# Tiled attention before a feed-forward chain: the last 192 queries of a head as two chunks of 96 on partition 0, products with v in one block per pair half

## The chip, the cores and the metric

The kernel runs on one core of a Trainium2 chip. The metric is the device time of one execution in microseconds (us). A core has TensorE (PE, which multiplies matrices, with a loader for its stationary operand, PEld), VectorE (DVE), ScalarE (ACT), GpSimd (POOL) and a DMA-issuing engine (SP). PE reads SBUF and writes PSUM, which has eight banks of 512 fp32 columns by 128 partitions.

## The reference

```python
def _attn_ref(q, k, v, s):            # 4 batches, 8 heads, 576 positions, head size 64
    scores = scale * np.matmul(q, k.transpose(0, 1, 3, 2))
    cum = np.cumsum(np.maximum(s, 0.0), axis=-1)
    bias = -(cum[:, :, :, None] - cum[:, :, None, :])
    scores = np.where(causal, -1000000000.0, scores + np.minimum(bias, 0.0))
    ...
    attn = attn / (np.sum(attn, axis=-1, keepdims=True) + 1e-09)
    return np.matmul(attn, v).astype(np.float32)

def reference(**kwargs):
    ...
    x = np.ascontiguousarray(attn_out.transpose(0, 2, 1, 3)).reshape(B * S, H * D)
    x = _moe_ref(x=x, **moe_kwargs)      # h = x @ w_in; (h - tanh(h)) @ w_out
    return _moe2_ref(x=x, **moe2_kwargs) # ((x @ w1) * (x @ w2) @ w3) @ w_out
```

## The kernel before

The first 440 us hold the attention, with half of the first feed-forward layer woven in, which ends near 490 us; the rest is feed-forward alone. Heads are worked in pairs (`Pair`): head e = 0 of a pair has its 64 components on partitions 0 to 63 of the tile `qk`, head e = 1 on 64 to 127. A pair half of kind "A" does queries 0 to 255, one of kind "B" queries 256 to 575. Queries are cut into five chunks, which begin at `CH0` = 0, 128, 256, 384, 448 and are 128 long. The fifth overlaps the fourth: only its rows from partition 64 on (`PLO`) are used, queries 512 to 575. A "B" half has three units (`UNITS`): B1 is chunk 3, B2 is chunk 4 with its first 512 keys, B3 is chunk 4's last 64 keys and chunk 2.

For each unit, `scores` multiplies queries by keys (per head one matmul with 64 contraction rows; PE runs each fp32 matmul as two passes), `minimum` adds the bias and takes a row's minimum on DVE, `exps` does the exponentials on ACT with row sums in `sums`. Seven steps later `transposes` turns the probabilities on PE, `BANKS` naming for each unit the key chunks and the query chunks whose blocks go side by side into a PSUM tile `pt`; `evacuate` copies it to the SBUF tile `pf`; `products` multiplies by v into the PSUM tile `pv`, head e = 0 into partitions 0 to 63 (64 stationary columns), e = 1 into 64 to 127. `invert`, `turn`, `store` and `spread` turn the reciprocals of the row sums (`ri`, 4 or 6 columns) on PE, write them to DRAM and read them back broadcast; `finish` multiplies `pv` by them into `xy`.

PSUM: the pool `ps_a` has five banks under one tag "s", shared by the scores, `pt`, `pv` and the turned reciprocals.

The order on PE is the order in which the code emits (`manual_schedule`). The function `at(step, order, fn)` fills a table of steps; each unit takes two steps, a pair (A and B) eight. In a step the transposes of one head come first, then `turn`, then scores, then feed-forward work (12 matmuls `h`, or 12 matmuls `y`, each of 256 columns), then `products`. Batch 0 comes first, four "A" halves, then four "B" halves; there (`p.first`) the bias and the mask are added on PE by extra matmuls, and exponentials read PSUM. Batches 1 to 3 follow as 12 pairs A, B. The other engines' order is chosen by the scheduler.

Of the kernel before, what the change touches and what calls it, by code (L numbers as in the profile page):

```python
# [8 lines left out]
F32 = mybir.dt.float32  # L9
# [21 lines left out]
CH0 = [0, 128, 256, 384, 448]  # L31
PLO = [0, 0, 0, 0, 64]
# [3 lines left out]
def tile_kernel(ctx: ExitStack, tc: tile.TileContext, qk, v, s, w_in, w_out, w1, w2, w3t, w_o2, outT):  # L36
# [65 lines left out]
    with ExitStack() as actx:  # L102
        def pool(name, bufs, **kw):
# [11 lines left out]
                 "B3": ((4, 512, S, 384), (2, 0, 384, 0))}  # L115
# [48 lines left out]
        def bias(p, i):  # L164
# [8 lines left out]
            if not p.first:  # L173
                t, lo, w = p.pr[i], PLO[i], min(P * (i + 1), S)
                for e in range(2):
                    c = cq[lo:, i, p.g[e]:p.g[e] + 1]
                    if i in (2, 3):
                        nc.gpsimd.tensor_scalar(out=t[lo:, e, :w], in0=p.cb[lo:, e, :w], scalar1=c, scalar2=0.0, op0=ALU.add, op1=ALU.min)  # L178
                    else:
                        nc.scalar.activation(t[lo:, e, :w], p.cb[lo:, e, :w], AF.Identity, bias=c)  # L180
# [6 lines left out]
        def causal(p, i):  # L187
            lo, w = PLO[i], min(P * (i + 1), S)
            dg = p.pr[i][lo:, :, P * i:w]
            nc.gpsimd.affine_select(out=dg, in_=dg, pattern=[[0, 2], [-1, w - P * i]], compare_op=ALU.is_ge,  # L190
                                    fill=-8e9, base=0, channel_multiplier=1)

        def scores(p, j):
            ps = [ps_a.tile([P, 512], F32, tag="s", name=f"s{p.n}_{j}_{e}") for e in range(2)]
            p.banks[j] = ps
            for i, k0, k1, o in UNITS[j]:
                for e in range(2):
                    x = p.raw[D * e:D * e + D]
                    latest[0] = nc.tensor.matmul(ps[e][:, o:o + k1 - k0], x[:, 0, CH0[i]:CH0[i] + P], x[:, 1, k0:k1],  # L199
                                                 start=(i, k0, k1, o) == UNITS[j][0] or not p.first, stop=not p.first, skip_group_check=p.first)  # L200
            if p.first:


                for e in range(2):
                    g = p.g[e]
                    todo = []
                    for i, k0, k1, o in UNITS[j]:
                        z, r = REL[i]
                        todo.append((ps[e][:, o:o + k1 - k0], pick[:, g:g + 1].broadcast_to([P, P]), rel2[z][:, r + k0:r + k1]))
# [6 lines left out]
        def minimum(p, j):  # L216
# [3 lines left out]
            if p.first:  # L220
                nm = p.nm
                for i, k0, k1, o in UNITS[j]:
                    lo = PLO[i]
                    c = 5 if i == 4 and not k0 else i
                    for e in range(2):
                        nc.vector.tensor_reduce(out=nm[lo:, e, c:c + 1], in_=p.banks[j][e][lo:, o:o + k1 - k0], op=ALU.max, axis=mybir.AxisListType.X)
                    if i == 4 and k0:
                        nc.vector.tensor_tensor(out=nm[lo:, :, 4:5], in0=nm[lo:, :, 4:5], in1=nm[lo:, :, 5:6], op=ALU.max)
                    if c < 5:
                        nc.vector.tensor_scalar(out=nm[lo:, :, c:c + 1], in0=nm[lo:, :, c:c + 1], scalar1=-0.125, scalar2=None, op0=ALU.mult)  # L230
                return
            for e in range(2):
                ps, nm = p.banks[j][e], p.nm[:, e]
                for i, k0, k1, o in UNITS[j]:
                    lo, t = PLO[i], p.pr[i][:, e]
                    part = i == 4 and not k0
                    nc.vector.tensor_tensor_reduce(  # L237
                        out=t[lo:, k0:k1], in0=ps[lo:, o:o + k1 - k0], in1=t[lo:, k0:k1], scale=-0.125,
                        scalar=nm[lo:, 5:6] if k0 else 3e38, op0=ALU.add, op1=ALU.min,
                        accum_out=nm[lo:, 5:6] if part else nm[lo:, i:i + 1])  # L240

        def exps(p, j):
            if p.sums is None:
                p.sums = a2.tile([P, 2, 4], F32, tag="sums", name=f"sums{p.n}", bufs=6)
                if not p.early:
                    nc.gpsimd.memset(p.sums[:D, :, 2:3], 1.0)
            for i, k0, k1, o in UNITS[j]:
                if i == 4 and not k0:
                    continue
                lo, c = PLO[i], i - p.i0  # L250
                for e in range(2):
                    t, m = p.pr[i][:, e], p.nm[lo:, e, i:i + 1]
                    if p.first:
                        if i == 4:
                            nc.scalar.activation(t[lo:, :512], p.banks["B2"][e][lo:, :512], AF.Exp, bias=m, scale=0.125, accum_out=p.sums[lo:, e, 3:4])  # L255
                        nc.scalar.activation(t[lo:, k0:k1], p.banks[j][e][lo:, o:o + k1 - k0], AF.Exp, bias=m, scale=0.125,
                                             accum_out=p.sums[lo:, e, c:c + 1])
                    else:
                        nc.scalar.activation(t[lo:, :], t[lo:, :], AF.Exp, bias=m, scale=-1.0, accum_out=p.sums[lo:, e, c:c + 1])  # L259
                if i == 4 and p.first:  # L260
                    nc.vector.tensor_add(p.sums[lo:, :, 2:3], p.sums[lo:, :, 2:3], p.sums[lo:, :, 3:4])

        def transposes(p, j, e):
            pt = ps_a.tile([P, 512], F32, tag="s", name=f"pt{p.n}_{j}_{e}")
            at, pieces = 0, []
            for kj, cs in BANKS[j]:
                beg = at
                for i in cs:
                    lo = PLO[i]
                    nc.tensor.transpose(pt[:, at:at + P - lo], p.pr[i][lo:, e, CH0[kj]:CH0[kj] + P], ident[lo:, lo:])  # L270
                    at += P - lo
# [9 lines left out]
        def products(p, j):  # L281
            got = [p.pf.pop((j, e)) for e in range(2)]
            if j in ("A", "B1"):
                if p.first and p.early:
                    p.pv = ps_y.tile([P, 512], F32, tag=f"y{p.n % 2}", name=f"pv{p.n}")
                else:
                    p.pv = ps_a.tile([P, 512], F32, tag="s", name=f"pv{p.n}")
            n = len(got[0][0])
            for z in range(n):
                for e in range(2):  # L290
                    kj, c, beg, end = got[e][0][z]
                    nc.tensor.matmul(p.pv[D * e:D * e + D, c:p.nq], p.vs[:, e, kj], got[e][1][:, beg:end],  # L292
                                     start=j in ("A", "B1") and z == 0, stop=j in ("A", "B3") and z == n - 1,
# [457 lines left out]
```

## Time and profile before

| what | value |
|---|---|
| runs | 1053.44, 1053.82, 1057.58 us, median 1053.82 |
| the profiled execution | 1053.08 us, its span 1051.3 us, mean granted TensorE clock 0.974 |
| busy of the span | PE 1001.3 us (95%), PEld 790.7 (75%), DVE 530.6 (50%), ACT 399.7 (38%), POOL 251.4 (24%) |
| the chain that ended last | PE 76%, DVE 10%, DMA 7%, ACT 4%, issue 2%, POOL 1% |
| transposes of the B halves (L270, `pt_B`) | 384 matmuls, 78.8 us busy |
| scores of the B halves (L199, `s_B`) | 256 matmuls, 64.1 us busy |

The span runs from the first to the last instruction, and the execution's own time is 1.8 us longer. Busy times of PE overlap from one matmul to the next, since matmuls are pipelined: what a matmul takes in a stream is read from the distance of the starts, not from its duration. The granted clock has two levels, 2.4 GHz (1.00) and 1.2 GHz (0.50); a mean over a stretch lies between.

### The profile page before, as it was taken

Reading aid. Unit: us, or ns where it says so; the run is one execution under the profiler, and the core shown is the slowest. Engines: PE = TensorE matmul, PEld = TensorE weight load, DVE = VectorE, ACT = ScalarE, POOL = GpSimd, SP = SyncE. Lnnn points to the kernel's source line nnn. Section 1 sums busy time; section 2 is a strip of 40 time slices with the busy share of each in tenths; the row PEclk is TensorE's granted clock in tenths of the full one; section 3 lists DMA queues with packets and bytes.
Section 4 is the critical chain, followed back from the end, with each engine's and each line's share of the span. In section 5 each row is a group of like instructions: output and inputs, shape, how many; then the busy total and the mean of one; then the engine's idle time right before and its main releaser. Section 6 shows DMA issues by size and latency. Waiting matters only on the chain.

```text
span 1051.3 us, 15383 instructions
## 1 busy us (share of the span) xinstructions
PE 1001.3 (95%) x5798; PEld 790.7 (75%) x5801; DVE 530.6 (50%) x1172; ACT 399.7 (38%) x978; POOL 251.4 (24%) x245
## 2 busy tenths in 40 slices
PE   6678799999999999999999999999999999999998
PEld 3345566666777777899877778888888888888898
DVE  8885554675555555553297674758412213122121
ACT  3454476765656564322233323223212112121121
POOL 3332365653333441100143321214101001000000
PEclk8978797999999999999999999999999999999999
DMA  6655664464222220205537453447910101001010
GB/s 208 208 183 203 206 186 135 152 194 140 91 77 91 83 92 14 69 21 167 175 120 240 160 196 99 165 141 269 363 70 1 41 0 41 1 1 41 1 41 21
DMA packets 46233, 123.64 MB, mean 118 GB/s; under 512 B 4976, under 2 KB 16912, under 8 KB 46160
## 3 DMA queue, kind: packets, MB, share of 16 engines
q1 hardware_dynamic: 41840, 106.94, 30.2%
q10 hardware_dynamic: 4320, 15.73, 4.5%
q8 instruction: 45, 0.74, 0.3%
q14 instruction: 28, 0.23, 0.1%
HBM read 92.09 MB, written 30.56 MB: 117 GB/s over the span
## 4 chain that ended last, share of the span: by engine, by line
PE 76%; DVE 10%; DMA 7%; ACT 4%; issue 2%; POOL 1%; SPq 0%; ACTq 0%; POOLq 0%; DVEq 0%
PE oc L98 9%; PE a L98 9%; PE b L98 9%; PE h L98 9%; PE y L391 8%; PE hb L98 6%; PE yb L98 6%; PE pt_B L270 5%; PE pv L292 4%; PE w3o L98 4%; PE s_B L199 3%; ACT pr L259 1%; DMA wf_d<-park_wout 1%; DVE cvt_w L76 1%; PE s_A L199 1%
## 5 line engine op out<-in xcount | busy, mean ns | idle before, releaser
L98 PEld LDWEIGHTS h<-xhl,win 128*128 128x128 f32 x864 | 110.0, 193 | 28.1 <-issue 14.1
L98 PE MATMUL h<-xhl,win 128*128 128x256 f32 x864 | 124.7, 292 | 2.9 <-DVE th L422 2.1
L698 DVE TENSOR_TENSOR pc<-b,pc 128x512 f32<-128x512 f32 (+1 forms) x40 | 25.5, 637 | 163.3 <-PE b L98 163.3
L98 PE MATMUL hb<-x,win 128*128 128x512 f32 (+1 forms) x480 | 106.3, 368 | 0.6 <-DMA win<-wf_d 0.6
L98 PE MATMUL a<-y,w 128*128 128x512 f32 (+1 forms) x480 | 106.4, 368 | 0.0
L98 PE MATMUL b<-y,w 128*128 128x512 f32 (+1 forms) x480 | 106.0, 368 | 0.0
L98 PE MATMUL yb<-ghb,wout 128*128 128x512 f32 (+1 forms) x320 | 97.3, 370 | 5.7 <-ACT ghb L60 3.8
L98 PE MATMUL oc<-phc,w3s 128*128 128x512 f32 (+1 forms) x320 | 96.7, 368 | 0.0
L98 PEld LDWEIGHTS hb<-x,win 128*128 128x128 f32 x480 | 84.0, 188 | 15.5 <-DMA win<-wf_d 0.8
L98 PEld LDWEIGHTS b<-y,w 128*128 128x128 f32 x480 | 84.3, 189 | 15.0
L98 PEld LDWEIGHTS a<-y,w 128*128 128x128 f32 x480 | 84.2, 189 | 14.9
L178 POOL TENSOR_SCALAR pr<-cb,cq 128x384 f32<-128x384 f32 (+1 forms) x48 | 85.9, 1807 | 21.5 <-PE pt_B L270 21.5
L270 PE MATMUL pt_B<-ident,pr 128*128 128x128 f32 (+1 forms) x384 | 78.8, 289 | 10.6 <-ACT pr L255 10.6
L391 PE MATMUL y<-gh,wout 128*128 128x256 f32 x576 | 88.2, 293 | 0.0
L391 PEld LDWEIGHTS y<-gh,wout 128*128 128x128 f32 x576 | 74.8, 193 | 8.3 <-issue 6.4
L259 ACT ACTIVATE pr<-pr,nm 128x128 f32<-128x128 f32 (+2 forms) x120 | 71.7, 598 | 21.4 <-DVE nm L237 20.0
L270 PEld LDWEIGHTS pt_B<-ident,pr 128*128 128x128 f32 (+1 forms) x384 | 46.0, 142 | 44.5 <-issue 24.4
L199 PE MATMUL s_B<-qk 64*128 64x512 f32 (+2 forms) x256 | 64.1, 543 | 9.4 <-DVE cq L552 4.5
L697 ACT COPY pc<-a 128x512 f32<-128x512 f32 (+1 forms) x40 | 21.8, 544 | 134.8 <-PE a L98 134.8
L61 POOL TENSOR_TENSOR y<-xy,y 128x512 fp32r<-128x512 f32 (+1 forms) x10 | 13.5, 1354 | 248.6 <-ACT y L60 248.4
L98 PEld LDWEIGHTS yb<-ghb,wout 128*128 128x128 f32 x320 | 58.5, 188 | 18.0 <-ACT ghb L60 4.7
L98 PEld LDWEIGHTS oc<-phc,w3s 128*128 128x128 f32 x320 | 58.5, 189 | 9.9
(128 smaller groups left out, 1631.5 us busy)
## 6 DMA issues: line engine op xcount, KB each, us to landing
qk<-in_qk SPq DMA_DIRECT2D x16, 576.0 KB
raw_w<-in_w3t SPq DMA_DIRECT2D x16, 512.0 KB
raw_w<-in_w SPq DMA_DIRECT2D x16, 512.0 KB
wg_d<-park_w SPq DMA_DIRECT2D x16, 512.0 KB
w<-wg_d SPq DMA_DIRECT2D x16, 512.0 KB
raw_win<-in_w_in ACTq DMA_DIRECT2D x15, 512.0 KB
raw_wout<-in_w_out ACTq DMA_DIRECT2D x15, 512.0 KB
cb<-cum_d SPq DMA_DIRECT2D x12, 576.0 KB
```

The source lines that it names most:

```text
L61: (lo or nc.gpsimd.tensor_sub)(dst_lo, src, dst_hi.bitcast(F32))
L76: nc.vector.scalar_tensor_tensor(out=t, in0=r3[:, :, 0], scalar=29, in1=t, op0=ALU.logical_shift_right, op1=ALU.bitwise_or)
L98: nc.tensor.matmul(ps, a, b, start=first and n == 0, stop=last and n == 2, skip_group_check=skip)
L178: nc.gpsimd.tensor_scalar(out=t[lo:, e, :w], in0=p.cb[lo:, e, :w], scalar1=c, scalar2=0.0, op0=ALU.add, op1=ALU.min)
L199: latest[0] = nc.tensor.matmul(ps[e][:, o:o + k1 - k0], x[:, 0, CH0[i]:CH0[i] + P], x[:, 1, k0:k1], start=(i, k0, k1, o) == UNITS[j][0] or ...
L259: nc.scalar.activation(t[lo:, :], t[lo:, :], AF.Exp, bias=m, scale=-1.0, accum_out=p.sums[lo:, e, c:c + 1])
L270: nc.tensor.transpose(pt[:, at:at + P - lo], p.pr[i][lo:, e, CH0[kj]:CH0[kj] + P], ident[lo:, lo:])
L292: nc.tensor.matmul(p.pv[D * e:D * e + D, c:p.nq], p.vs[:, e, kj], got[e][1][:, beg:end], start=j in ("A", "B1") and z == 0, stop=j in ("A" ...
L391: nc.tensor.matmul(o, wout[f][:, z, P * c:P * c + P], x, start=f == 0 and n == 0 and c % 2 == 0, stop=f == F1 - 1 and n == 2, skip_group_c ...
L697: nc.scalar.copy(t[:, :n], pa[:, :n])
L698: nc.vector.tensor_mul(t[:, :n], pb[:, :n], t[:, :n])
```

## The change

The fourth and fifth chunk become queries 384 to 479 and 480 to 575, each 96 long and each from partition 0 (`PW` is a chunk's length, `KC0` the key chunks, which stay at 0, 128, 256, 384, 448). Wherever a slice ran from `lo` to 128 it now runs from 0 to `pw`. In B3 chunk 2 is now done ahead of chunk 4's last keys. `products` does nothing until the last unit of a half and then issues all of the half's matmuls in one block, so `pv` is taken later, and `pf` tiles are held longer: instead of one ring of four there are three rings of two, A and B3 sharing one. The reciprocals are transposed as 96 columns, of which 4 or 6 are in use. In batch 0, B2 gets a mask matmul of 32 columns per head, since chunk 4's diagonal now begins at key 480. `queries` scales in two instructions instead of one.

```diff
-CH0 = [0, 128, 256, 384, 448]
-PLO = [0, 0, 0, 0, 64]
+CH0 = [0, 128, 256, 384, 480]
+PW = [128, 128, 128, 96, 96]
+
+KC0 = [0, 128, 256, 384, 448]
...
-                 "B3": ((4, 512, S, 384), (2, 0, 384, 0))}
+                 "B3": ((2, 0, 384, 0), (4, 512, S, 384))}
...
-                    latest[0] = nc.tensor.matmul(ps[e][:, o:o + k1 - k0], x[:, 0, CH0[i]:CH0[i] + P], x[:, 1, k0:k1],
+                    latest[0] = nc.tensor.matmul(ps[e][:PW[i], o:o + k1 - k0], x[:, 0, CH0[i]:CH0[i] + PW[i]], x[:, 1, k0:k1],
...
-                        if k1 == min(P * (i + 1), S):
-                            lo = PLO[i]
-                            todo.append((ps[e][:, o + P * i - k0:o + k1 - k0], identb, maskb[:, lo:]))
+                        pw, d = PW[i], max(k0, CH0[i])
...
+                        if d < k1:
+                            todo.append((ps[e][:pw, o + d - k0:o + k1 - k0], identb[:, :pw], maskb[:, d - CH0[i]:k1 - CH0[i]]))
...
-                    lo = PLO[i]
-                    nc.tensor.transpose(pt[:, at:at + P - lo], p.pr[i][lo:, e, CH0[kj]:CH0[kj] + P], ident[lo:, lo:])
-                    at += P - lo
+                    pw = PW[i]
+                    nc.tensor.transpose(pt[:, at:at + pw], p.pr[i][:pw, e, KC0[kj]:KC0[kj] + P], ident[:pw, :pw])
+                    at += pw
...
-            pf = a2.tile([P, 512], F32, tag="pf", name=f"pf{p.n}_{j}_{e}", bufs=4)
+            pf = a2.tile([P, {"B1": 512, "B2": 416}.get(j, 384)], F32, tag=f"pf{0 if j == 'A' else j[1]}".replace("3", "0"), name=f"pf{p.n}_{j}_{e}")
...
         def products(p, j):
-            got = [p.pf.pop((j, e)) for e in range(2)]
-            if j in ("A", "B1"):
-                if p.first and p.early:
...
+            if j != p.units[-1]:
+                return
...
+            todo = []
+            for u in p.units:
+                got = [p.pf.pop((u, e)) for e in range(2)]
+                for z in range(len(got[0][0])):
+                    todo.append([got[e][0][z] + (got[e][1],) for e in range(2)])
+            for z, both in enumerate(todo):
+                for e, (kj, c, beg, end, pf) in enumerate(both):
+                    nc.tensor.matmul(p.pv[D * e:D * e + D, c:p.nq], p.vs[:, e, kj], pf[:, beg:end],
+                                     start=z == 0, stop=z == len(todo) - 1, skip_group_check=True)
...
-            p.ri = a2.tile([P, 2, p.ni], F32, tag="ri", name=f"ri{p.n}", bufs=4)
+            p.rw = rws[p.n % 4]
+            p.ri = p.rw[:, :2 * p.ni].rearrange("p (t i) -> p t i", t=2)
...
-            nc.tensor.transpose(p.pt[:2 * p.ni, :P], p.ri.rearrange("p t i -> p (t i)"), ident)
+            nc.tensor.transpose(p.pt[:PW[4], :P], p.rw, ident)
...
-            nc.vector.tensor_scalar(out=cq, in0=pt[:, :5 * NH].rearrange("p (i g) -> p i g", g=NH), scalar1=-1.0, scalar2=None, op0=ALU.mult)
+            for i0, i1 in ((0, 3), (3, 5)):
```

On PE, the first head's transposes of unit B1 of a later pair, up to the feed-forward matmuls, before and after (`pr_3` and `pr_4` are the probabilities of chunks 3 and 4, the shape at the end is that of the output):

```order
L270 MATMUL pt_B_0_3319<-ident,pr_2_3124 128x128
L270 MATMUL pt_B_0_3319<-ident,pr_3_2941 128x128
L270 MATMUL pt_B_0_3319<-ident,pr_4_3036 128x64
L270 MATMUL pt_B_0_3319<-ident,pr_3_2941 128x128
L270 MATMUL pt_B_0_3319<-ident,pr_4_3036 128x64
L303 MATMUL pri_3325<-ident,ri_3279 6x128
L391 MATMUL y_3_3168<-gh_2_3222,wout_474 128x256 x2
```

```order
L272 MATMUL pt_B_0_3314<-ident,pr_2_3115 128x128
L272 MATMUL pt_B_0_3314<-ident,pr_3_2939 128x96
L272 MATMUL pt_B_0_3314<-ident,pr_4_3033 128x96
L272 MATMUL pt_B_0_3314<-ident,pr_3_2939 128x96
L272 MATMUL pt_B_0_3314<-ident,pr_4_3033 128x96
L309 MATMUL pri_3320<-ident,rw_96 96x128
L402 MATMUL y_3_3159<-gh_2_3209,wout_480 128x256 x2
```

The order is the same; the blocks from 64 rows (output 128x64) and from 128 rows have become blocks from 96 rows.

On PE, the end of unit B2 and of unit B3 of the same pair, before (`pv` is the product with v):

```order
L391 MATMUL y_3_3169<-gl_0_3057,wout_230 128x256 x2
L292 MATMUL pv_3095<-pf_B_0_3104,vs_2527 64x320
L292 MATMUL pv_3095<-pf_B_1_3159,vs_2527 64x320
L292 MATMUL pv_3095<-pf_B_0_3104,vs_2527 64x64
L292 MATMUL pv_3095<-pf_B_1_3159,vs_2527 64x64
L270 MATMUL pt_B_1_3188<-ident,pr_2_2785 128x128
...
L391 MATMUL y_3_3169<-gl_1_3152,wout_349 128x256 x2
L292 MATMUL pv_3095<-pf_B_0_3186,vs_2527 64x320
L292 MATMUL pv_3095<-pf_B_1_3235,vs_2527 64x320
L270 MATMUL pt_A_3264<-ident,pr_1_2865 128x128 x3
```

and now:

```order
L402 MATMUL y_3_3160<-gl_0_3053,wout_237 128x256 x2
L272 MATMUL pt_B_1_3175<-ident,pr_2_2778 128x128
...
L402 MATMUL y_3_3160<-gl_1_3143,wout_354 128x256 x2
L298 MATMUL pv_3247<-pf_B_0_3018,vs_2518 64x320
L298 MATMUL pv_3247<-pf_B_1_3061,vs_2518 64x320
L298 MATMUL pv_3247<-pf_B_0_3018,vs_2518 64x192
...
L298 MATMUL pv_3247<-pf_B_1_3222,vs_2518 64x320
L272 MATMUL pt_A_3260<-ident,pr_1_2854 128x128 x3
```

The products of B1 and B2 have left their places behind `y` and stand, ten in a row, where those of B3 alone stood.

On ACT, in batch 0, around the exponentials of unit B3 of one pair and the copies of an earlier pair's transposed blocks, before:

```order
L255 ACTIVATE pr_4_570,sums_614<-s_B_0_643,nm_602 64x512
L256 ACTIVATE pr_4_570,sums_614<-s_B_0_690,nm_602 64x64
L255 ACTIVATE pr_4_570,sums_614<-s_B_1_644,nm_602 64x512
L256 ACTIVATE pr_4_570,sums_614<-s_B_1_691,nm_602 64x64
L256 ACTIVATE pr_2_649,sums_614<-s_B_0_690,nm_602 128x384
L256 ACTIVATE pr_2_649,sums_614<-s_B_1_691,nm_602 128x384
L278 COPY pf_B_0_767<-pt_B_0_735 128x320
```

and now:

```order
L281 COPY pf_B_0_766<-pt_B_0_738 128x320
L258 ACTIVATE pr_2_657,sums_620<-s_B_0_693,nm_608 128x384
L258 ACTIVATE pr_2_657,sums_620<-s_B_1_694,nm_608 128x384
L62 CAST gh_1_726<-th_1_725 128x256
L257 ACTIVATE pr_4_577,sums_620<-s_B_0_649,nm_608 96x512
L258 ACTIVATE pr_4_577,sums_620<-s_B_0_693,nm_608 96x64
L257 ACTIVATE pr_4_577,sums_620<-s_B_1_650,nm_608 96x512
```

The copy of that block now stands ahead of the exponentials instead of behind them.

## Rows read from the trace of the kernel before

**Rows 1.** Windows: busy us of PE, PEld, DVE, ACT, POOL, granted clock, DMA share, GB/s.
```profile
0.00:139.30 139.30, 107.11 (x586) 64.05 (x589) 101.64 (x220) 65.65 (x192) 50.38 (x58) 0.85 0.60 198
...
163.00:187.30 24.30, 24.30 (x157) 16.02 (x155) 11.30 (x40) 15.34 (x42) 11.62 (x13) 0.86 0.43 142
...
299.71:323.94 24.23, 24.23 (x182) 17.91 (x181) 13.36 (x49) 13.66 (x39) 9.03 (x11) 1.00 0.25 77
```

**Rows 2.** Waits of PE, 0 to 480: total us, times, longest.
```profile
PE pt_B L270 <- ACT pr L255: 10.6, 3, 5.1
...
PE s_B L199 <- DVE cq L552: 4.5, 1, 4.5
PE s_B L199 <- ACT pf_B L278: 4.3, 3, 3.3
...
PE h L98 <- DVE th L422: 2.1, 1, 2.1
```

**Rows 3.** Timeline of PE in one pair: start, length of a merged group.
```profile
299.71 1.05 PE L270 MATMUL pt_B<-ident,pr 128*128 128x128 f32 x5
...
300.72 1.19 PE L391 MATMUL y<-gh,wout 128*128 128x256 f32 x8
...
303.11 1.10 PE L270 MATMUL pt_B<-ident,pr 128*128 128x128 f32 x5
...
305.06 1.66 PE L98 MATMUL h<-xhl,win 128*128 128x256 f32 x12
306.55 0.64 PE L270 MATMUL pt_B<-ident,pr 128*128 128x128 f32 x4
...
307.15 1.17 PE L391 MATMUL y<-gh,wout 128*128 128x256 f32 x8
...
308.71 1.08 PE L292 MATMUL pv<-pf_B,vs 128*64 128x320 f32 x8
309.72 0.64 PE L270 MATMUL pt_B<-ident,pr 128*128 128x128 f32 x3
...
310.20 0.22 PE L270 MATMUL pt_B<-ident,pr 64*128 64x64 f32 x1
...
311.27 1.66 PE L98 MATMUL h<-xhl,win 128*128 128x256 f32 x12
312.76 0.58 PE L270 MATMUL pt_B<-ident,pr 128*128 128x128 f32 x3
313.27 1.19 PE L391 MATMUL y<-gh,wout 128*128 128x256 f32 x8
...
314.85 0.87 PE L292 MATMUL pv<-pf_B,vs 128*64 128x320 f32 x8
315.65 0.64 PE L270 MATMUL pt_B<-ident,pr 128*128 128x128 f32 x3
...
317.14 1.65 PE L98 MATMUL h<-xhl,win 128*128 128x256 f32 x12
318.63 0.49 PE L270 MATMUL pt_A<-ident,pr 128*128 128x128 f32 x3
318.88 1.17 PE L391 MATMUL y<-gh,wout 128*128 128x256 f32 x8
...
320.43 0.76 PE L292 MATMUL pv<-pf_B,vs 128*64 128x320 f32 x4
321.12 0.55 PE L270 MATMUL pt_A<-ident,pr 128*128 128x128 f32 x3
```

**Rows 4.** Timeline of PE in narrow windows, one transpose each (names: rows*columns).
```profile
299.82 0.27 PE L270 MATMUL pt_B<-ident,pr 128*128 128x128 f32 x1
300.03 0.27 PE L270 MATMUL pt_B<-ident,pr 64*128 64x64 f32 x1
300.23 0.33 PE L270 MATMUL pt_B<-ident,pr 128*128 128x128 f32 x1
```

**Rows 5.** The same view, one pass of `pv` with both heads each.
```profile
309.46 0.33 PE L292 MATMUL pv<-pf_B,vs 128*64 128x192 f32 x2
```

More of the change, by code (lines that the diff above doesn't have):

```diff
@@ L187, in causal @@
         def causal(p, i):
[L188 to L190 removed]
+            c, w = CH0[i], min(P * (i + 1), S)
+            dg = p.pr[i][:PW[i], :, c:w]
+            nc.gpsimd.affine_select(out=dg, in_=dg, pattern=[[0, 2], [-1, w - c]], compare_op=ALU.is_ge,
                                     fill=-8e9, base=0, channel_multiplier=1)
@@ L281, in products @@
         def products(p, j):
-            got = [p.pf.pop((j, e)) for e in range(2)]
-            if j in ("A", "B1"):
-                if p.first and p.early:
[L285 to L293, printed above, removed]
-                                     skip_group_check=True)
+            if j != p.units[-1]:
+                return
+            if p.first and p.early:
+                p.pv = ps_y.tile([P, 512], F32, tag=f"y{p.n % 2}", name=f"pv{p.n}")
+            else:
+                p.pv = ps_a.tile([P, 512], F32, tag="s", name=f"pv{p.n}")
+            todo = []
[7 more added lines that the diff above has]
+                                     start=z == 0, stop=z == len(todo) - 1, skip_group_check=True)
         def invert(p):
-            p.ri = a2.tile([P, 2, p.ni], F32, tag="ri", name=f"ri{p.n}", bufs=4)
+            p.rw = rws[p.n % 4]
+            p.ri = p.rw[:, :2 * p.ni].rearrange("p (t i) -> p t i", t=2)
             nc.vector.tensor_scalar(out=p.ri, in0=p.sums[:, :, :p.ni], scalar1=1e-9, scalar2=None, op0=ALU.add)
@@ L316, in spread @@
                 nc.sync.dma_start(p.rb[D * e:D * e + D, :w], p.rd[e:e + 1, :w].broadcast_to([D, w]))
+        rws = [cp.tile([P, PW[4]], F32, tag=f"rw{z}", name=f"rw{z}") for z in range(4)]
+        for z in range(4):
+            nc.gpsimd.memset(rws[z], 0.0)
         written = [0] * B
         def finish(p):
-            for q, z, r in ((p.q0, min(p.q0 + p.nq, 512), 0), (512, p.q0 + p.nq, BLK + D)):
+            for q, z, r in ((p.q0, min(p.q0 + p.nq, CH0[4]), 0), (CH0[4], p.q0 + p.nq, BLK)):
                 if q < z:
@@ L550, in queries @@
             for i in range(5):
-                nc.tensor.transpose(pt[:, NH * i:NH * i + NH], cum[:, CH0[i]:CH0[i] + P], ident[:NH, :NH])
-            nc.vector.tensor_scalar(out=cq, in0=pt[:, :5 * NH].rearrange("p (i g) -> p i g", g=NH), scalar1=-1.0, scalar2=None, op0=ALU.mult)
+                nc.tensor.transpose(pt[:PW[i], NH * i:NH * i + NH], cum[:, CH0[i]:CH0[i] + PW[i]], ident[:NH, :NH])
+            for i0, i1 in ((0, 3), (3, 5)):
+                pw = PW[i0]
+                nc.vector.tensor_scalar(out=cq[:pw, i0:i1], in0=pt[:pw, NH * i0:NH * i1].rearrange("p (i g) -> p i g", g=NH),
+                                        scalar1=-1.0, scalar2=None, op0=ALU.mult)
         at(12, 5.2, queries)
```

46 lines of the change are left out of this document (23 added, 23 removed).

## The prediction

> **What bounds the kernel now.** Read the windows first [rows 1]. The attention falls into two parts. In the 12 pairs of batches 1 to 3 PE is busy 24.23 of 24.23 us of a pair, at the full clock from 187 us on, while ACT has 13.66, DVE 13.36 and POOL 9.03: PE is the bound, and a pair costs what its matmuls cost in a row. Batch 0 (up to 139.3 us) is mixed: PE 107.11 of 139.30, DVE 101.64, at a mean clock of 0.85, which is 0.30 of the stretch, some 41 us, at 1.2 GHz. Then the waits [rows 2]: the longest of PE in the attention are 10.6 us of transposes for ACT's exponentials of chunk 4 (line 255) and 4.5 and 4.3 us of scores for DVE and ACT, all in batch 0. What follows the attention is not touched and is PE's own; it moves with the attention's end.
>
> Since durations overlap, I read costs from distances of starts. Three single transposes [rows 4] with the group that begins at 299.71 [rows 3] give the key: 128 rows to 128 rows 0.11 us, 128 rows to 64 rows 0.21, 64 rows back to 128 rows 0.20. A three-transpose run from 128 rows throughout takes 0.25 up to the start of `y` (318.63 to 318.88), since the matmul behind a run is recorded some 0.03 after the run's last start. So a crossing between 64 rows and 128 rows costs 0.09 to 0.10 beyond the 0.11 of the transpose, and a transpose of 64 columns is no cheaper than one of 128.
>
> The Trainium skill says why in "TensorEngine Tiling (Array Packing)", Key Properties: changing the tiling mode drains TensorE. The rows agree, with 0.09 us for each change. The same list says that tiles of one mode run in parallel, and this speaks against the change.
>
> How much would be lost by that? Where 64-row transposes of the second head precede scores, which also use 64 rows, they do run beside them: the transpose at 310.20 lies inside the scores [rows 3]. Four such transposes per pair (one in B1, two in B2, one in B3) at 0.11 are 0.44 us per pair, 5.3 us in 12 pairs, that the change gives up. The working below uses the distances as they stand, with that overlap in them, so it is already paid.
>
> **The change, part by part**, for one pair at full clock [rows 3]. A full-array transpose counts 0.11 (0.109 unrounded, a third of the run above plus the 0.03), the last one before scores 0.20, for the crossing that remains. Scores of 512 columns alone count 0.95: two passes at the 0.109 per 128 columns of the transposes, that is 2 x 0.43, and a crossing back.
>
> - First head of B1: 299.71 to 300.72 is 1.01 us with the reciprocals' transpose; after, five at 0.109 and 0.03: 0.58. Gain 0.43.
> - Second head of B1 with its scores: 303.11 to 305.06, 1.95. After: 0.165 (the first transpose behind products has always this extra), three at 0.109, 0.20, 0.95: 1.65. Gain 0.30.
> - First head of B2: 306.55 to 307.15, 0.60; after, four and 0.03: 0.47. Gain 0.13.
> - Second head of B2: 309.72 to 311.27, 1.55; after, three at 0.109, 0.20, 0.95: 1.48. Gain 0.07.
> - First head of B3: 312.76 to 313.27, 0.51; after, as the run of three: 0.25. Gain 0.26.
> - Second head of B3: 315.65 to 317.14, 1.49; after, two at 0.109, 0.20, and scores of 384 and 64 columns, which I count 0.95 as well (the 64-column passes at 0.11, no cheaper than 128 columns): 1.37. Gain 0.12.
> - Products: 308.71 to 309.72 (1.01), 314.85 to 315.65 (0.80), 320.43 to 321.12 (0.69): 2.50. A pass of 192 columns and the exit took 0.26 (309.46 [rows 5] to 309.72), of which 0.16 is columns; so 0.10 is the exit, paid three times now. The first block's 1.01 is 0.87 of columns (two passes of 320 and of 192) and this exit, which leaves 0.05 ahead of it. One block saves two exits and two of these, 0.30, and pays 32 more columns in two passes, 0.05. The entries (about 0.09 each, by the crossing) are another 0.18. Gain 0.43.
>
> Sum: 1.74 us per pair, 20.9 us in 12 pairs. A check by counting along both orders from the end of batch 0 on: 365 changes between 128 rows, 64 rows and 64 columns become 148; 217 at 0.094 are 20.4.
>
> What costs nothing: the reciprocals' transposition as 96 columns instead of 4 or 6. Its row moves 128 columns before and after, in the 0.11 of a transpose whose weights are 128 wide. Bounds: nothing, and 0.09 gained on each of 32 if the narrow one is a mode of its own (2.9 us); I take nothing, since behind the pair's run with it the `y` starts as soon as without (the 0.03 above). DVE, ACT and POOL instructions change partitions more than columns; the wider copies (416 for 384) and masks on POOL hide under PE's 24.23 us, and would cost their 0.1 us or so per pair if PE were not the bound.
>
> **Batch 0.** 90 changes become 43; 47 at 0.094 are 4.4 us at full clock and up to twice that at half. PE is busy three quarters of the time there, so I take 3 (bounds 0 and 8). The banks: today `pv` holds one of five from B1's products to `finish`, scores of B2 and B3 hold four, so the next transposes wait for ACT's exponentials of B2 to free one; that is the wait of 10.6 us in three pieces. Now `pv` comes last, the fifth bank is free, and ACT's copy of that block stands ahead of the exponentials instead of behind. What is late next is the `y` behind it, whose operand comes from the same ACT and POOL round, then the second head's transposes. I take a quarter, 2.7 us (bounds 0 and 10.6). Against this, eight more mask matmuls with their weight loads, about 0.1 each, 0.8, and the second scaling in `queries`, 0.3 on top of the wait of 4.5 us.
>
> In all 20.9 + 3 + 2.7 - 1.1 = 25.5 us off the profiled execution's 1053.08 us (span 1051.3 and 1.8 around it): 1027.6. The median of the runs shown is 0.7 above that execution, so I say 1028 for a median.
>
> **The rivals.**
>
> *The clock of the first 187 us moves.* Some 41 us lie at half clock in batch 0 and about 7 in the window from 163 us (clock 0.86) [rows 1], and more between them. PE-bound work loses half of such time. If the bank waits vanish and the clock falls less often with them, a third of it could go: 7 us more, and with all 10.6 us of waits gone some 1013. If a stretch of 14 us is added and batch 0 yields nothing, 1028 + 5 + 7 = 1040. For the first: fewer waits. For the second: shorter matmul runs leave more waiting for DVE, which has 101.64 of 139.30. I give 0.10 to either.
>
> *96 rows behave as a mode of their own.* No matmul of the trace has 96 rows. If changing from 128 to 96 rows cost the 0.094 too, each first-head run pays two crossings and each second-head run one more: 3 x 0.19 + 3 x 0.09 = 0.85 per pair, 10 us in all: 1038. Against it: every shape of over 64 rows in the trace is 128. Chance 0.06.
>
> The Trainium skill's page "TensorEngine Tiling (Array Packing)", Available Configurations, lists row tiles of 128, 64 and 32 alone, so that by it 96 rows run as 128; no run here shows it yet.
>
> *Slower: ACT waits for the block.* A and B3 share a ring of two `pf` tiles. The copy of the next A's first head must now wait for the block of products in the same step, and everything behind that copy on ACT (exponentials, the tanh of `h`) with it; PE then waits for the DVE subtraction that frees the one bank of `h`, a wait of which the trace has one of 2.1 us [rows 2]. It decides once it costs over 2.1 us per pair (25.5 by 12); at 2.6 in each of 12 pairs, 31 us, the time is 1059. Against it: ACT is idle 10.6 of 24.23 us, the block itself is only some 2.25 us long, so a single wait for all of it would just reach the point. Chance 0.02.
>
> *The gain is swallowed*: PE shortened by 7% uncovers chains through ACT and DVE in every step, and the pair stays near 24 us; 1048 to 1054. Against it: PE's waits in the 12 pairs are now few, and the other engines need 14 us of a pair. Chance 0.03.
>
> **How the numbers follow.** Forecast (pairs near 22.4 us, batch 0 a few us shorter) 0.69, clock either way 0.20, 96 rows 0.06, swallowed 0.03, slower 0.02. The likeliest is 1028, its own range 1020 to 1035, from the bounds of batch 0. With the clock and the other cases the range is 1013 to 1038, which leaves out the tails of the clock's two cases and the last three. A measurement of this kernel can tell about 0.5%, 5 us. Faster by more than that: 0.95; within it: 0.03; slower: 0.02.
>
> **What would show it.** In the timeline, B-half transposes should start 0.11 apart throughout, with about 0.20 only before scores and none of 0.20 inside a run; the block of ten products (twenty matmuls) should last 2.25 us; the same place of the next pair should come 22.4 to 22.6 us later, at PE busy throughout. The wait of `pt_B` for line 255's successor should be gone from the list of waits or under 5 us. From the attention's end on, everything should be as before, only earlier. The prediction is wrong if starts of 96-row transposes are over 0.15 apart, if PE gets idle time inside the pairs, or if half clock returns after 187 us.

## The result, and the profile after

The changed kernel takes 1027.74 us (median of four runs, 1026.97 to 1030.51) against 1053.72 us of the kernel before: ratio 0.9752, interval [0.9717, 0.9788], 26 us faster. In a later comparison it came to 1030.17 us at a ratio of 0.9807 [0.977, 0.9843]. The profiled execution took 1030.51 us, its span is 1028.2 us.

Windows of the changed kernel, cut where batch 1's first scores `s_A` begin, five pairs later, at one pair, and at the last stage (busy us of PE, PEld, DVE, ACT, POOL, then granted clock, DMA share, GB/s):

```profile
0.00:124.10 124.10, 92.69 (x537) 59.04 (x537) 93.94 (x203) 57.91 (x169) 44.28 (x54) 0.85 0.65 214
124.10:236.70 112.60, 103.78 (x758) 78.25 (x758) 66.32 (x222) 78.81 (x226) 70.19 (x72) 0.94 0.53 176
...
304.04:326.60 22.56, 22.56 (x181) 18.13 (x180) 14.33 (x51) 15.52 (x45) 9.25 (x12) 1.00 0.32 106
727.10:1028.10 301.00, 297.31 (x1454) 252.13 (x1452) 67.52 (x105) 58.82 (x106) 10.47 (x8) 1.00 0.09 35
```

The same cuts in the kernel before:

```profile
0.00:132.40 132.40, 100.20 (x540) 59.62 (x543) 99.09 (x208) 59.70 (x175) 43.81 (x50) 0.85 0.61 201
132.40:246.70 114.30, 110.49 (x742) 75.68 (x741) 64.56 (x209) 77.54 (x212) 67.13 (x71) 0.94 0.53 173
...
750.10:1051.20 301.10, 297.31 (x1454) 252.13 (x1452) 67.51 (x105) 58.81 (x106) 10.47 (x8) 1.00 0.10 35
```

Batch 0 has lost 8.3 us, the first five pairs 1.7 us, and the last stage nothing. In the first two windows the mean clock is the same, 0.85 and 0.94. In the trace's clock records PE stood at half clock for 41.0 us of batch 0 before and 37.5 us after, and for 13.7 us of the five pairs in both, so the clock can have given at most some 2 us. PE's busy time in the five pairs fell by 6.7 us, yet only 1.7 us came out: PE now waits there. One profile scatters by some us, though. The later comparison (below, `after_again`) left a second profile of the same kernel, in which batch 1 begins at 124.4 us and the five pairs take 109.9 us with 6.8 us at half clock, 4.4 us less than before. The rest came from the later pairs, which the timeline of PE shows (start, length of a merged group; it answers to [rows 3]):

```profile
281.59 0.93 PE L201 MATMUL s_A<-qk 64*128 64x128 f32 x8
...
283.97 0.60 PE L272 MATMUL pt_B<-ident,pr 128*128 128x128 f32 x5
284.41 0.28 PE L309 MATMUL pri<-ident,rw 128*96 128x128 f32 x1
284.44 1.19 PE L402 MATMUL y<-gh,wout 128*128 128x256 f32 x8
...
286.83 0.67 PE L272 MATMUL pt_B<-ident,pr 128*128 128x128 f32 x5
287.43 1.10 PE L201 MATMUL s_B<-qk 64*96 64x512 f32 x4
288.46 1.68 PE L100 MATMUL h<-xhl,win 128*128 128x256 f32 x12
289.98 0.52 PE L272 MATMUL pt_B<-ident,pr 128*128 128x128 f32 x4
...
290.37 1.19 PE L402 MATMUL y<-gh,wout 128*128 128x256 f32 x8
...
291.87 0.52 PE L272 MATMUL pt_B<-ident,pr 128*128 128x128 f32 x4
...
293.35 1.69 PE L100 MATMUL h<-xhl,win 128*128 128x256 f32 x12
294.87 0.44 PE L272 MATMUL pt_B<-ident,pr 128*128 128x128 f32 x3
295.09 1.19 PE L402 MATMUL y<-gh,wout 128*128 128x256 f32 x8
...
296.60 0.44 PE L272 MATMUL pt_B<-ident,pr 128*128 128x128 f32 x3
...
297.95 1.69 PE L100 MATMUL h<-xhl,win 128*128 128x256 f32 x12
...
301.31 2.33 PE L298 MATMUL pv<-pf_B,vs 128*64 128x320 f32 x20
303.57 0.55 PE L272 MATMUL pt_A<-ident,pr 128*128 128x128 f32 x3
304.04 0.93 PE L201 MATMUL s_A<-qk 64*128 64x128 f32 x8
```

From one `s_A` to the next, 281.59 to 304.04, are 22.45 us where a pair took 24.23 [rows 1]. The run that began at 299.71 and reached `y` 1.01 us later [rows 3] now reaches it in 0.47 (283.97 to 284.44). Narrow windows on that run, the first start, then the starts that are left as the window moves on, show 0.11 behind the one transpose of 128 columns and 0.08 behind each of 96 (284.08, 284.25 two transposes later, 284.41 for `pri` two more):

```profile
283.97 0.27 PE L272 MATMUL pt_B<-ident,pr 128*128 128x128 f32 x1
...
284.08 0.41 PE L272 MATMUL pt_B<-ident,pr 96*128 96x96 f32 x3
284.25 0.33 PE L272 MATMUL pt_B<-ident,pr 96*128 96x96 f32 x2
```

The waits of PE up to 480 us (total us, times, longest; they answer to [rows 2]); the first line, 8.0 us for `pri`, left out here, lies in the first 21 us of the kernel, where the one before waits 6.3 us:

```profile
...
PE h L100 <- DVE th L433: 7.1, 5, 3.0
PE s_B L201 <- ACT pr L257: 6.7, 3, 4.1
PE s_B L201 <- issue: 4.6, 1, 4.6
PE s_A L201 <- ACT pf_B L281: 3.4, 1, 3.4
...
```

The transposes' wait of 10.6 us for the exponentials of chunk 4 is gone; the scores behind them now wait for the same exponentials (6.7 us), and `h` waits 7.1 us for DVE where it waited 2.1. Of these 7.1 us, 5.0 lie in the first five pairs, and the longest, 3.0 us, can be followed back. `h` waits for DVE's subtraction `th`, this for ACT's tanh `th`, and ACT had been idle for 4.78 us behind a load that is issued from its queue (ACTq), that of one of the weight tiles that are only parked for the second half:

```profile
164.53 0.33 ACTq L67 DMA_DIRECT2D raw_win<-in_w_in  x1
164.97 0.38 ACT L430 ACTIVATE th<-h 128x256 f32<-128x256 f32 x1 [4.78 <-issue]
...
165.39 0.42 DVE L433 TENSOR_TENSOR th<-h,th 128x256 f32<-128x256 f32 x1 [3.39 <-ACT th L430]
...
165.86 0.58 PE L100 MATMUL h<-xhl,win 128*128 128x256 f32 x1 [3.04 <-DVE th L433]
```

The queue's instruction ahead of that load waits from 157.8 us on for 6.66 us. In the second profile it waits 5.33 us, until the tile loaded before has landed, and `h` then waits 1.7 us.

### The profile page after: what moved, and what is told of

Same layout as the page of the kernel before. It is cut to its first block, busy times and chain, and to the rows that moved or that the text cites. A ratio compares the mean times of both kernels' runs of the same rounds, so it can differ in the third digit from the quotient of the medians.

```text
span 1028.2 us, 15378 instructions
## 1 busy us (share of the span) xinstructions
PE 974.8 (95%) x5809; PEld 795.6 (77%) x5809; DVE 524.5 (51%) x1173; ACT 394.7 (38%) x978; POOL 253.8 (25%) x249
## 4 chain that ended last, share of the span: by engine, by line
PE 49%; DVE 6%; DMA 3%; ACT 1%; issue 1%; POOL 0%; SPq 0%; ACTq 0%; POOLq 0%; DVEq 0%
PE oc L100 10%; PE a L100 10%; PE b L100 10%; PE hb L100 6%; PE yb L100 6%; PE w3o L100 4%; PE h L100 2%; PE y L402 2%; DVE cvt_w L78 1%; DVE glb L63 1%; DVE x L63 1%; DMA raw_w<-in_w3t 1%; DVE cvt_w L76 1%; DMA win<-wf_d 1%; DVE cvt_wo L78 1%
## 5 line engine op out<-in xcount | busy, mean ns | idle before, releaser
L100 PE MATMUL h<-xhl,win 128*128 128x256 f32 x864 | 126.8, 293 | 8.5 <-DVE th L433 7.1
L201 PE MATMUL s_B<-qk 64*96 64x512 f32 (+2 forms) x256 | 60.2, 531 | 12.2 <-ACT pr L257 6.7
L100 PE MATMUL yb<-glb,wout 128*128 128x512 f32 (+1 forms) x160 | 59.7, 377 | 1.7 <-DVE glb L63 1.7
L62 ACT CAST phc<-pc 128x512 fp32r<-128x512 f32 (+1 forms) x40 | 23.1, 578 | 93.2 <-DVE pc L712 93.2
```

The costliest lines, as they stand in the source:

```text
L62: (hi or nc.scalar.copy)(dst_hi, src)
L100: nc.tensor.matmul(ps, a, b, start=first and n == 0, stop=last and n == 2, skip_group_check=skip)
L201: latest[0] = nc.tensor.matmul(ps[e][:PW[i], o:o + k1 - k0], x[:, 0, CH0[i]:CH0[i] + PW[i]], x[:, 1, k0:k1], start=(i, k0, k1, o) == UNITS ...
```

## Experiments

**One part alone: the block of products.** The kernel before, with the changed `products` and its rings.

```diff
 (before)
-            got = [p.pf.pop((j, e)) for e in range(2)]
+            if j != p.units[-1]:
+                return
...
+            for u in p.units:
+                got = [p.pf.pop((u, e)) for e in range(2)]
```

> The kernel before with the products of a half in one block (and the three rings of two for the transposed probabilities), chunks and transposes as before. Theory (changes of tiling mode are the price): per pair two entries, two exits, two extra passes and two slower first transposes less, about 0.6 us, 7 us in 12 pairs, and in batch 0 the part of the gain that comes from the freed bank (some 5 of the 8 us seen there): 1040 to 1046, at a pair spacing of 23.6 us. Rival (the freed bank and the later products are the whole gain): near 1030, at a pair spacing near 22.5. Rival (the block gives nothing): 1052 to 1055.

Measured: 1037.45 us, ratio 0.9851 [0.98, 0.9902]. Timeline of PE, two `s_A` in a row, 23.66 us apart, and the windows of batch 0 and the five pairs:

```profile
282.19 0.93 PE L199 MATMUL s_A<-qk 64*128 64x128 f32 x8
...
305.85 0.93 PE L199 MATMUL s_A<-qk 64*128 64x128 f32 x8
```

```profile
0.00:121.30 121.30, 96.58 (x525) 57.94 (x528) 94.72 (x198) 56.96 (x164) 40.67 (x48) 0.86 0.64 205
121.30:234.80 113.50, 109.24 (x756) 76.48 (x756) 70.47 (x223) 83.47 (x231) 71.28 (x74) 0.94 0.54 189
```

The block is worth 0.57 us per pair, and 11.1 us in batch 0, more than the whole change has there. In the five pairs it gains 0.8 us. The total came 2.5 us below the range of the theory, which had counted on some 5 us in batch 0. Neither rival fits.

**The other part alone: chunks of 96.** The changed kernel with the products of each unit in their place and the old ring of four.

```diff
 (after)
+            got = [p.pf.pop((j, e)) for e in range(2)]
...
-            if j != p.units[-1]:
-                return
```

> The changed kernel with the products of each unit in their old places (and the old ring of four), chunks of 96 kept. Theory: of the 1.78 us per pair about 1.2 stay, 14 us in 12 pairs, less what batch 0 gained from the bank: 1036 to 1042, pair spacing near 23.05 us, and the transposes of a later pair wait for exponentials again in batch 0. Rival (chunks of 96 give all that changed by PE time): 1028 to 1031, spacing 22.5. Rival (they give nothing and the block is the gain): 1050 or more.

Measured: 1038.04 us, ratio 0.9853 [0.9809, 0.9896]. Two `s_A` in a row, 23.05 us apart:

```profile
284.51 0.93 PE L201 MATMUL s_A<-qk 64*128 64x128 f32 x8
...
307.56 0.93 PE L201 MATMUL s_A<-qk 64*128 64x128 f32 x8
```

Its windows:

```profile
0.00:135.20 135.20, 100.77 (x551) 63.53 (x554) 99.75 (x218) 61.70 (x179) 50.77 (x59) 0.82 0.67 221
135.20:238.40 103.20, 99.75 (x741) 73.07 (x740) 59.55 (x204) 74.83 (x215) 63.13 (x67) 0.98 0.48 159
```

The chunks are worth 1.18 us per pair, and cost 2.8 us in batch 0. The two parts add up: 0.57 + 1.18 = 1.75 of 1.78 us per pair, and -11.1 + 2.8 = -8.3 us in batch 0, which is what the whole change has. In the total they do not add up (16 to 17 us each alone, 26 together), and the place is the first five pairs: there the chunks alone gain 11.1 us (103.2 for 114.3) and the block alone 0.8, but both together 1.7 (4.4 in the second profile). The clock has a part in this: half clock for 4.6 us of the five pairs here, 13.7 us in the kernel before and in the first profile of the changed one. The wait of the transposes for the exponentials of chunk 4 is here, as expected, since `pv` takes its bank early:

```profile
PE pt_B L272 <- ACT pr L257: 11.1, 3, 4.6
```

**The narrow transposition of the reciprocals.**

```diff
 (after)
-            nc.tensor.transpose(p.pt[:PW[4], :P], p.rw, ident)
+            nc.tensor.transpose(p.pt[:2 * p.ni, :P], p.rw[:, :2 * p.ni], ident)
```

> The changed kernel with the reciprocals transposed as 4 or 6 columns again. Theory (a narrow stationary operand is no mode of its own as far as time goes): no change, 1026.5 to 1029.5. Rival (it is a mode and costs two changes each time): 0.19 us for each of 32, and 24 of them inside the pairs, so 4.5 us or more on top: 1032 to 1034, pair spacing 22.8 instead of 22.45.

Measured: 1026.96 us, ratio 0.9749 [0.9714, 0.9784]; `s_A` starts at 280.81 and 303.27, 22.46 us apart. The padding is worth nothing, as forecast.

**The bank taken early.**

```diff
 (after)
-            if j != p.units[-1]:
-                return
-            if p.first and p.early:
+            if j in ("A", "B1"):
...
+                    if j == "B1":
+                        nc.vector.memset(p.pv[:, :1], 0.0)
+            if j != p.units[-1]:
+                return
```

> The changed kernel, but the PSUM bank of a B half's products is taken where it was before (a one-column fill by VectorE at the end of B1 holds it), the block of products stays last. Theory (the gain of batch 0 beyond mode changes is the bank): 3 to 6 us slower than the changed kernel, 1031 to 1034, all of it before 130 us; the wait of transposes for the exponentials of chunk 4 comes back with 5 us or more. Rival (the bank is beside the point): 1027 to 1029. In the pairs both expect 22.45 to 22.6 us.

Measured: 1025.57 us, ratio 0.9743 [0.9706, 0.978]: no slower. Waits of PE in its batch 0, and its windows:

```profile
PE pt_B L272 <- ACT pr L257: 9.3, 3, 3.9
```

```profile
0.00:127.40 127.40, 96.71 (x533) 62.30 (x536) 94.57 (x209) 59.35 (x174) 46.12 (x54) 0.81 0.65 208
127.40:234.40 107.00, 102.30 (x757) 75.87 (x756) 67.42 (x225) 77.24 (x220) 68.19 (x73) 0.98 0.56 185
```

The wait came back as the theory has it and batch 0 got 3.3 us longer, but the next five pairs took 107.0 us instead of 112.6. The total lies outside both ranges, below the rival's. The theory holds for its place and fails for the total. Part of what moved is half clock: 10 us more of it in batch 0 and 10 us less in the five pairs, 51.2 us up to the sixth pair in both kernels. So the 3.3 us are not the bank's alone.

**Parking late.** In the steps up to the sixth pair the other engines also convert 16 weight tiles that are parked in DRAM for the second half. Here their loads wait for PE's step, in the changed kernel and in the one before, and they are issued from SyncE's queue instead of ACT's.

```diff
 (after, and the same in before)
-            raws = [load_raw(*late[0][2:], nc.scalar)]
+            raws = [load_raw(*late[0][2:], nc.sync, after=latest[0])]
...
+        if after is not None:
+            tc.add_manual_dep(i.ins, after.ins.name, mybir.DependencyInfo(
+                mybir.DependencyClass.Sync, mybir.DependencyReason.DATA))
```

> The changed kernel, but the loads of the 16 weight tiles that are only parked (converted and written back for the second half) wait for the score matmul of the step in which the code asks for them, on SyncE's queue, so that their conversions come after 200 us instead of between 70 and 220 us. Theory (up to the end of the parking the time is set by this conversion work, which stands in the same queues of VectorE, ScalarE and GpSimd as the attention; so the gain of the first five pairs was swallowed there): the five pairs take 100 to 105 us instead of 112.6, batch 0 gets no longer, 1016 to 1023. Rival (the waits in the first five pairs are the attention's own): 1026 to 1030, the five pairs 111 to 114 us.

> The kernel before with the same late parking. Theory (its first five pairs, 114.3 us, were bound more by PE than those of the changed kernel): it gains less than the changed kernel does by the same edit, 1044 to 1051, and the difference of the two becomes 26 to 32 us, that is the changes of mode over all 12 pairs and part of batch 0. Rival (the parking costs both the same): both move by the same amount, or neither does.

Measured: 1024.16 us, ratio 0.9711 [0.9682, 0.9741], and 1050.61 us, ratio 0.997 [0.9944, 0.9997]. Windows of the changed kernel with late parking (batch 0, four pairs, the fifth pair), then of the kernel before with it:

```profile
0.00:114.30 114.30, 89.29 (x533) 57.47 (x536) 78.36 (x175) 53.07 (x161) 33.30 (x46) 0.88 0.47 145
114.30:195.30 81.00, 78.63 (x590) 58.94 (x590) 39.67 (x151) 58.45 (x173) 45.90 (x51) 0.96 0.34 112
195.30:219.90 24.60, 23.06 (x169) 17.55 (x168) 17.26 (x51) 16.73 (x48) 14.27 (x16) 0.93 0.66 225
```

```profile
0.00:125.80 125.80, 100.09 (x540) 59.20 (x543) 78.65 (x178) 55.15 (x167) 34.35 (x42) 0.84 0.42 131
125.80:209.30 83.50, 81.82 (x574) 55.71 (x574) 37.83 (x140) 56.44 (x158) 43.78 (x51) 0.99 0.34 108
209.30:238.50 29.20, 27.51 (x170) 19.09 (x170) 19.34 (x59) 20.03 (x57) 14.55 (x15) 0.82 0.50 172
```

By the sixth pair the changed kernel is 16.8 us ahead of where it was (219.9 for 236.7), the kernel before only 8.2 (238.5 for 246.7). Up to there the change gains 18.6 us instead of 10.0 (12.4 with the second profile), 7.1 of them in the five pairs, which take 105.6 us where 100 to 105 was expected.

That the parking took the change's gain there is shown in part only. In the first four pairs, in which no parked tile is converted now until their last 5 us, both kernels became faster, from 90.0 us (87.2 in the second profile) to 80.9 and from 90.7 to 83.5, so the parking slows both. But the change gains only 2.6 us there, where 7.0 was forecast. The changed kernel stands at half clock for 6.8 us of these four pairs and the one before for 1.5 us, which accounts for some 2.7 us of the difference, if PE loses half of such time. The other 4.5 of the 7.1 us lie in the fifth pair, in which the late conversions run in both (DVE begins them at 190.4 and 206.5 us) and the kernel before stands at half clock for 10.2 us.

The conversions then slow the later pairs, on average 24.3 us each instead of 22.5 in the changed kernel and 25.3 instead of 24.6 in the one before, and the two totals fell by about the same, 3.6 and 3.8 us against the medians of the unchanged kernels. So for the totals the second expectation's rival was right, although 1050.61 and the difference of 26.4 us lie in its theory's ranges; 1024.16 lies between the ranges of the first expectation.

**Merged blocks.** The products of a B half two steps later, right ahead of the next A half's, with a ring for B3 and narrow reciprocals.

```diff
 (after)
-                at(k + lag + 2, 8, products, p, j)
+                at(k + lag + 2 + (2 * joined if j == p.units[-1] else 0), 8, products, p, j)
...
-            fin = ke + lag + 3
+            fin = ke + lag + 3 + 2 * joined
```

> The changed kernel with the products of a B half moved two steps on, right ahead of those of the next A half, so that both make one block (12 blocks fewer), with a ring of its own for B3 and the narrow transposition of the reciprocals. Theory (a block of products costs an entry, an exit, a slower first pass and a slower transpose behind it, 0.30 us): pair spacing 22.15 instead of 22.45 us, 1022 to 1025. Rival (the price of the separate blocks was somewhere else, or the longer block makes ScalarE's copies late): 22.45 or more, 1027 to 1030.

Measured: 1023.46 us, ratio 0.971 [0.9681, 0.9739]. Two `s_A` in a row:

```profile
278.19 0.93 PE L201 MATMUL s_A<-qk 64*128 64x128 f32 x8
...
300.26 0.93 PE L201 MATMUL s_A<-qk 64*128 64x128 f32 x8
```

The spacing is 22.07 us here and 22.07 to 22.30 over the later pairs, on average 22.16 where the changed kernel has 22.47: a block less per pair is worth about the 0.30 us of the theory.

**Chunk 4's exponentials first.** In batch 0, B3's maxima and exponentials in the old order.

```diff
 (after)
-                for i, k0, k1, o in UNITS[j]:
+                for i, k0, k1, o in UNITS[j][::-1 if j == "B3" else 1]:
...
-            for i, k0, k1, o in UNITS[j]:
+            for i, k0, k1, o in UNITS[j][::-1 if j == "B3" and p.first else 1]:
```

> The changed kernel with the maxima and exponentials of B3 in batch 0 in the old order (chunk 4 ahead of chunk 2), the score matmuls in the new one. Theory (the profile of chunks96_only reached batch 1 2.8 us later than the kernel before, since chunk 4's exponentials, which give two PSUM banks back, now stand behind chunk 2's): batch 0 gets 2 to 4 us shorter than the 124.1 us of the changed kernel, the total 1023 to 1027. Rival (the order is hidden, the later start has another cause, or the first five pairs take the gain back): 1026 to 1029 and batch 0 at 122 to 126 us.

Measured: 1020.42 us, ratio 0.97 [0.9656, 0.9743]; `s_A` of batch 1 begins at 121.0 us in its profile, 3.0 earlier. Both kernels were then run again side by side:

> The changed kernel once more, next to the one with chunk 4's exponentials first, on one chip. If that order is worth something: 1025.5 to 1029 here and 3 us or more above the other; the place where batch 1 begins again within 2 us of 124. If its 1020.4 was the luck of its chip and day (the kernel before also ran 2 us lower there): both within 2 us of each other.

> Chunk 4's maxima and exponentials first, once more. If the order is worth something: 1019 to 1024, batch 1 begins 2 to 4 us ahead of the changed kernel's. If not: 1025.5 to 1028.

Measured: 1030.17 us, ratio 0.9807 [0.977, 0.9843], and 1021.67 us, ratio 0.9722 [0.9692, 0.9751]. The intervals do not touch: the order is worth some 8 us in this pair of runs (7 between the first measurements), more than the 3 us that it moves batch 0. Windows of the second pair of runs, from the end of the woven feed-forward to the last stage, the changed kernel and then this one:

```profile
491.30:725.10 233.80, 226.05 (x1059) 187.62 (x1058) 159.86 (x219) 77.68 (x143) 68.09 (x50) 0.99 0.53 183
```

```profile
488.00:719.00 231.00, 223.32 (x1059) 185.15 (x1058) 158.82 (x219) 77.52 (x143) 67.58 (x50) 1.00 0.54 185
```

3 us were gained in batch 0, almost none in the pairs that follow, and 2.8 in this window, where the changed kernel stood at half clock for 6.8 us. That the order saved those 2.8 is not shown: its own first profile has 3.4 us of half clock at the same place. These are single profiled executions; the rest of the 8 us is not placed.

**Both on top of the merged blocks.** Neither adds to them:

> The merged blocks and that order together. Theory: another 1 to 3 us below the merged blocks' 1023.5, so 1020 to 1023, pair spacing 22.15 us as there. Rival (the first five pairs take back what batch 0 gains): 1022.5 to 1025.

> The merged blocks and the late parking together. If the conversions cost the same wherever they stand while PE has little slack: late parking gave 3.6 us on the changed kernel by taking some 17 us off the time up to the sixth pair and giving 13 back later; with pairs of 22.15 us it gives back more, 1020 to 1023. If the two gains are independent: 1019 to 1020.5. If the merged blocks already used the slack: 1023 or more.

Measured: 1024.09 us, ratio 0.9738 [0.9697, 0.9779], and 1024.2 us, ratio 0.9733 [0.9691, 0.9776]. With chunk 4 first, batch 1 began at 113.1 us, but the five pairs took 119.6 us:

```profile
113.10:232.70 119.60, 104.00 (x744) 78.89 (x744) 68.02 (x224) 80.80 (x231) 70.61 (x73) 0.91 0.54 183
```

The first rival was right: the gain of batch 0 is taken back. The second is above all its ranges but the last. So the best version that was run is the changed kernel with chunk 4's exponentials first, 1020.4 and 1021.7 us; it beats both kernels.

## Why the prediction was right, step by step

*The cause, and the sum over the pairs.* Right. Forecast 1.74 us per pair, measured 1.78 at full clock (24.23 to 22.45). Piece by piece, forecast and measured distance from the rows above: first head of B1 0.58 and 0.47, of B2 0.47 and 0.39, of B3 0.25 and 0.22; second head with scores 1.65 and 1.63, 1.48 and 1.48, 1.37 and 1.35; the block of products 2.25 and 2.26. Two terms were off and cancelled in the second heads. A transpose of 96 columns takes 0.08, not 0.11: the sentence that a transpose of 64 columns is no cheaper than one of 128 was true of the rows that it was read from, but no ground to count 96 columns as 128. And scores of 512 columns take 1.03 (287.43 to 288.46), not 0.95: the forecast left out that the first pass of a pair of heads is longer than its columns. The one-part experiments show both halves of the cause, 0.57 for the block (forecast 0.43 and the slower transposes behind, counted with the second heads) and 1.18 for the chunks.

The price of 0.109 for a transpose does not follow from the working given for it (a third of 0.25 and 0.03 are 0.113), but the starts do lie 0.11 apart, so nothing hangs on it. The pieces hide a third term. Added up they measure 7.80 us where 8.05 was forecast, 0.25 better, and yet the pair is only 0.04 better. The matmuls that the forecast held unchanged became longer: twelve `h` take 1.52 to 1.53 (282.45 to 283.97) where they took 1.49 (305.06 to 306.55 [rows 3]), four times a pair, and `y` a little, 0.18 together; and the two entries into products that went saved 0.13 instead of 0.18. `chunks96_only` has the longer `h` too and `block_only` does not; why was not tested.

The prediction's check by counting changes of tiling agreed too well. Counted in the trace, there are 360 changes from batch 1 on if the narrow transposition of the reciprocals counts as 64 columns, and 335 if not; after the change there are 148. The 25 cost nothing, as the experiment on them shows, so the check should have read 187 at 0.094, that is 17.6 us. In a settled pair 26 changes become 12, and 14 at 0.094 are 1.3 of the 1.78 us. The rest is, by an estimate from the distances above, 18 transposes at 0.08 instead of 0.11 (0.5) and two slow first transposes less (0.1), against the longer `h` and `y` (0.2).

*All 12 pairs.* Here the sum failed, by 7 us: the first five pairs gave 1.7 us instead of 8.7 (4.4 in the second profile). PE was the bound there before (110.49 of 114.30 busy), and after the change it is not (103.78 of 112.60). Idle time of PE inside the pairs is one of the prediction's own signs of being wrong. It is also the rival of the swallowed gain, held to have a chance of 0.03 for the whole, in a part of the pairs. What took the gain is shown in part: the longest wait, 3.0 of the 8.8 us that PE is idle there, hangs on the load of a parked tile in ACT's queue; the next longest wait of `h`, 1.5 us before 209.35 us, follows one of 4.0 us of ACT for the DMA that loads `cb`, the sums from which the bias is made. Late parking speeds up these pairs in both kernels, in the changed one by more, but it moves the loads to another queue as well, so it does not tell the hold on ACT from the work of converting. The forecast looked at one late pair, in which ACT, DVE and POOL have room, and took it for all.

*Batch 0.* Mis-sized the other way: 8.3 us instead of 4.6 (3 + 2.7 - 1.1). The block alone gives 11.1 and the chunks take 2.8. The freed bank was the right mechanism for the wait of 10.6 us (gone, and back at 9.3 when the bank is held, 11.1 with the old products). It moved batch 0 by 3.3 us, near the 2.7, though with 10 us more of half clock; for the total it is worth nothing, since the five pairs take it back. What the chunks cost was seen in part: besides the extra mask matmuls, the new order of B3 puts the exponentials that free two banks behind two others, a cost of 3.0 us in batch 0 by the experiment that turns it round. The prediction had shown that order and not priced it.

*Reciprocals.* Nothing, as forecast.

*The rivals.* The clock hardly moved in the first 240 us of the first profile (0.85 and 0.94 in both kernels); in the second PE stood at half clock for 40.9 us up to the sixth pair, which began 2.4 us earlier than in the first with its 51.2 us; the kernel before has 54.7 us. So this rival took part in the size of the gain, by a few us. The half clock also came back after 187 us, another sign of being wrong that the prediction names: between 494 and 727 us the changed kernel lost 2.7 us against the kernel before (233.0 and 230.3 us), with 6.8 us at half clock. 96 rows are no mode of their own: changes from 128 to 96 rows cost nothing (0.11, then 0.08). ACT does wait for the block of products before it copies the next A half's blocks, 1.7 to 1.9 us in each settled pair, but PE is busy throughout those pairs (22.56 of 22.56), so it costs nothing there.

So the total was right by a price per pair that was right where it was read, a count of pairs that was 7 us too high and a batch 0 that was 4 us too low. The forecast was 20.9 + 4.6; measured were in the first two profiled executions 8.3 up to batch 1, 1.7 in the five pairs, 12.9 over the six distances from the sixth pair to the last (246.73 to 394.42 us before, 236.68 to 371.52 after: 1.78 each, and 2.1 more in the first), 2.8 from there to the end of the woven feed-forward, and 2.7 lost behind it with the half clock. That is 23.0 of the 23.1 us between the spans; the profiled execution of the changed kernel lies 2.8 above its median. That the total is within 1 us is partly luck.

How much the time up to the sixth pair is set by something other than PE can be read from all the runs with early parking that have the block or the chunks: batch 1 began anywhere from 113.1 to 135.2 us, and the sixth pair from 230.8 to 238.4. It is not all of it: with the chunks alone PE is busy for 99.75 of the 103.20 us of the five pairs, and the last parked tile is written back at 189.5 us, 49 us ahead of the sixth pair. Apart from the hold on ACT's queue, which shows in both profiles of the changed kernel and in neither of its parts alone, which engine or transfer sets the time was not told apart.

## What to carry to other kernels

Where PE is the bound, price a matmul by the distance to the next start and look at the shape of its neighbours: changes between row and column tilings cost some 0.09 us each here, so sort the work by tiling, even if a block gets padded for it. A gain on PE counts only while PE is the bound, so check a sum over a loop in its first rounds as well as in a settled one. When a loop's order is changed, price what the order frees (banks, rings), not only what it runs.

## What was not expected of the hardware

- An fp32 transpose with 128 stationary columns follows another after 0.08 us when 96 columns move, and after 0.11 us when 128 move, so its weight load does not hold it at 0.11.
- The reciprocals' transposition with 4 or 6 stationary columns takes no more time than with 96 (22.46 and 22.45 us per pair).
- A load issued from ACT's queue holds ACT back while it waits: 6.66 us at the queue, 4.78 us of them idle on ACT, and 3.04 us idle on PE two steps on.
- The clock fell to half for 6.8 us at 554.6 us in the changed kernel, in a stage whose instructions are those of before, during a wait of PE of 3.0 us for ACT. The kernel before has such a wait of 3.1 us (up to 580.8) and stays at full clock. Of the 14 profiled executions 11 have a half clock of 3.4 to 6.8 us between 548 and 582 us, one of them the kernel before with late parking; the profiles of the kernel before, of the chunks alone and the second one with chunk 4 first have none:

```profile
554.60:561.40 6.80, 6.17 (x15) 4.81 (x16) 4.87 (x9) 2.32 (x4) 1.28 (x1) 0.50 0.69 229
```
